# Eight row buffers and a new order for the first eight units in a linear-attention and feed-forward kernel

## The chip, the cores and the metric

The kernel runs on one core of one Trainium2 chip. The metric is the device time of one execution in microseconds (us). A core has engines that run side by side and wait for each other by semaphores: TensorE (PE, matmuls; its weight loads are listed as PEld), VectorE (DVE), ScalarE (ACT), GpSimd (POOL) and SyncE (SP, which only issues transfers here). Every engine works its own instructions off in the order in which the program has them, so an instruction that waits holds up all that stand behind it on that engine.

## The reference

There are two parts. The first is a linear attention with a decaying state: per batch b (4) and head h (8), over 768 steps of 48 channels, with a decay w per channel and a bonus u for the present step. The second is a feed-forward layer with a SiLU between two matrices of 384 x 2048 and 2048 x 384, on all 3072 tokens.

```python
for t in range(S):
    kt, vt, rt = (k[:, :, t].copy(), v[:, :, t].copy(), r[:, :, t].copy())
    cur = np.einsum('bhd,bhe->bhde', u[None] * kt, vt)
    y[:, :, t] = np.einsum('bhd,bhde->bhe', rt, state + cur)
    state = w[None, :, :, None] * state + np.einsum('bhd,bhe->bhde', kt, vt)
...
h = x @ w_in
g = h * (1.0 / (1.0 + np.exp(-h)))
return (g @ w_out).astype(np.float32)
```

## The kernel before

The sequence is cut into six chunks of 128 steps. A *unit* is one chunk of one batch, 24 in all; units 0 to 3 are chunk 0 of the four batches, 4 to 7 chunk 1, and so on. One unit loads the rows of r, k and v (three transfers), turns r and k on TensorE, multiplies them by powers of the decay on VectorE (`rT`, `kT`), forms their product (the 128 x 128 scores of eight heads), masks it (`am`), multiplies it by v (`yp`), adds the bonus part (`vu`) while it leaves PSUM, and updates the state of its batch. When the four batches of a chunk are done, the chunk passes through the feed-forward layer: `hps` is the first layer, `gT` its SiLU, `ops` the second layer.

The row buffers, the loads and the PSUM tiles:

```python
    NIN = 4

    ...
        return divmod(i, B)

    att = [ps.tile([128, 2, 512], FP, name=f"att{i}") for i in range(2)]
    turns = []

    def next_att():
        turns.append(0)
        return att[len(turns) % 2]

    ...
    u_bc = cst.tile([128, H, D], FP)
    rin = [big.tile([128, H, 64], FP, name=f"rin{i}") for i in range(NIN)]
    kin = [big.tile([128, H, 64], FP, name=f"kin{i}") for i in range(NIN)]
    vin = [big.tile([128, H, D], FP, name=f"vin{i}") for i in range(NIN)]
    ...
    wout = big.tile([128, NFT, HD], F16)

    def ld(i, dst, src, eng=nc.sync):
        sc, b = unit(i)
        eng.dma_start(
```

A load of rows is cut into runs of 48 numbers. The first transfers, the zero matmuls (`spin`, they write zeros over a tile that is about to be used and only keep TensorE busy) and the way in which u reaches all partitions:

```python
    columns(nc.sync, wpT, w, 1)
    columns(nc.scalar, wpT, w, 0)
    nc.scalar.dma_start(out=u_row, in_=bass.AP(tensor=u.tensor, offset=0, ap=[[0, 1], [1, HD]]))
    nc.scalar.dma_start(out=w_row, in_=bass.AP(tensor=w.tensor, offset=0, ap=[[0, 1], [1, HD]]))
    for i in range(B):
        for dst, src in ((rin, r), (kin, k), (vin, v)):
            ld(i, dst, src, nc.scalar if i < 2 and dst is kin else nc.sync)
    nc.vector.memset(ones, 1.0)
    ...
    spins = [0]

    def spin(ps_tile):
        for _ in range(spins[0]):
            nc.tensor.matmul(ps_tile, idle[:, 0:128], idle[:, 0:ps_tile.shape[-1]],
                             start=True, stop=True)
        spins[0] = 0
    ...

    def spread_row(key, row):
        spread[key] = ps.tile([128, HD], FP, name="bc", tag="moe", bufs=4)
        nc.tensor.matmul(spread[key], ones, row, start=True, stop=True)
    ...
    def copy_u():
        nc.scalar.copy(out=u_bc.rearrange("p h d -> p (h d)"), in_=spread["u"])
        nc.scalar.copy(out=maskX[0:HC, :], in_=maskM[HC:C, :])
        nc.scalar.copy(out=maskX[HC:C, :], in_=maskM[0:HC, :])
```

The bonus is the sum over channels of r times k times u, times v. `bonus_ku` and `bonus_rku` are on GpSimd, `bonus_sum` on VectorE; `bonus_v_rows` is used for units 0 to 3, `bonus_v` for the others:

```python
    def bonus_ku(i):
        L(i)["ku"] = wrk.tile([128, H, D], FP, name="ku")
        nc.gpsimd.tensor_tensor(out=L(i)["ku"], in0=kin[i % NIN][:, :, 0:D], in1=u_bc, op=ALU.mult)

    def bonus_rku(i):
        L(i)["rku_f"] = wrk.tile([128, H, D], FP, name="rku_f")
        nc.gpsimd.tensor_tensor(out=L(i)["rku_f"], in0=rin[i % NIN][:, :, 0:D], in1=L(i)["ku"],
                                op=ALU.mult)

    def decayed_k(i):
        nc.gpsimd.tensor_tensor(out=kc[i % NIN][:, :, 0:D], in0=kin[i % NIN][:, :, 0:D],
                                in1=lamC, op=ALU.mult)

    def bonus_v_rows(i):
        L(i)["vu"] = wrk.tile([128, H, D], FP, name="vu")
        nc.vector.tensor_tensor(out=L(i)["vu"], in0=vin[i % NIN],
                                in1=L(i)["rku"].unsqueeze(2).broadcast_to([128, H, D]),
                                op=ALU.mult)
    ...
    def bonus_v(i):
        L(i)["vu"] = wrk.tile([128, H, D], FP, name="vu")
        nc.gpsimd.tensor_tensor(out=L(i)["vu"], in0=vin[i % NIN],
                                in1=L(i)["rku"].unsqueeze(2).broadcast_to([128, H, D]),
                                op=ALU.mult)
    ...
    def turn_one(i, x):
        if x == 0:
            t = next_att()
            spin(t[:, 0, :])
            L(i)["t"] = t.rearrange("p y (x g t) -> p y x g t", x=2, g=NP)
        else:
            spin(L(i)["t"][:, 0, 1].rearrange("p g t -> p (g t)"))
        flat = (rin, kin)[x][i % NIN].rearrange("p h d -> p (h d)")
        for p in range(NP):
            for y in range(2):
                rows = slice(HC * y, HC * y + HC)
                nc.tensor.transpose(L(i)["t"][0:PR, y, x, p, :], flat[rows, 128 * p:128 * p + PR],
                                    ident[rows, rows])

    ...
        L(i)[key] = wrk.tile([PR, NP, C], FP, name=key)
        nc.vector.tensor_tensor(
            out=L(i)[key].rearrange("p g (y t) -> p y g t", y=2),
            in0=L(i)["t"][0:PR, :, x], in1=lam.rearrange("p g (y t) -> p y g t", y=2),
            op=ALU.mult)
```

The product, the mask, the output, the state and the first layer. All PSUM tiles with the tag "moe" (`bc`, `yp`, `sp`, `yT`, `hps`, `ops`) rotate through four buffers; the two `att` tiles are used in turn:

```python
    def product(i):
        at = next_att()
        spin(at[:, 0, :])
        a = L(i)["a"] = at.rearrange("p j (g c) -> p j g c", g=NP)
        rT, kT = L(i)["rT"], L(i)["kT"]
        for p in range(NP):
            for j, r0 in ((0, 0), (1, 64)):
                nc.tensor.matmul(a[:, j, p, :], kT[r0:r0 + D, p, :], rT[r0:r0 + D, p, :],
                                 start=True, stop=True)
    ...
        nc.vector.tensor_tensor(
            out=am.rearrange("p h g c -> p (h g) c"), in0=L(i)["a"].rearrange("p h g c -> p (h g) c"),
            in1=(maskX if crossed(i) else maskM).unsqueeze(1).broadcast_to([128, H, C]), op=ALU.mult)
    ...
        yp = ps.tile([128, 512], FP, name="yp", tag="moe", bufs=4)
        spin(yp)
        L(i)["y"] = yp[:, 0:HD].rearrange("p (h d) -> p h d", h=H)
    ...
        L(i)["sp"] = ps.tile([128, 512], FP, name="sp", tag="moe", bufs=4)
        L(i)["sps"] = L(i)["sp"][:, 0:HD].rearrange("p (g n) -> p g n", g=NP)
        kf = kc[i % NIN].rearrange("p h d -> p (h d)")
        vf = L(i)["v16"].rearrange("p h d -> p (h d)")
        for p in range(NP):
            nc.tensor.matmul(L(i)["sps"][:, p, :], kf[:, 128 * p:128 * p + 128],
                             vf[:, PW * p:PW * p + PW], start=True, stop=True)
    ...
        nc.vector.tensor_tensor(out=L(i)["y16"], in0=L(i)["y"], in1=L(i)["vu"], op=ALU.add)
    ...
            if sc:
                nc.vector.tensor_tensor(out=dst, in0=src,
                                        in1=L(i)["sdec"][p0:p0 + D, :, c0:c0 + D], op=ALU.add)
            else:
                nc.scalar.copy(out=st16[b][p0:p0 + D, :, c0:c0 + D], in_=src)
                nc.scalar.copy(out=dst, in_=src)
    ...
        hps = hpss[b0, ft] = ps.tile([128, m, nb * C], FP, name="hps", tag="moe", bufs=4)
        spin(hps.rearrange("p m c -> p (m c)"))
        for f in range(m):
            for q in range(NQ):
                nc.tensor.matmul(hps[:, f, :], win[:, q, (ft + f) * 128:(ft + f + 1) * 128],
                                 xts[sc][:, q, b0:b0 + nb, :].rearrange("p b t -> p (b t)"),
                                 start=(q == 0), stop=(q == NQ - 1))
    ...
        nc.scalar.activation(out=gts[sc][:, ft:ft + m, b0 * C:(b0 + nb) * C], in_=hpss[b0, ft],
                             func=AF.Silu)
```

The first eight units follow a written list, in which every word is one of the steps above with the number of its unit (`TR`, `TK`: turn r, k; `ku`, `ru`, `rd`: the three steps of the bonus; `S`: the state's matmuls; `yT`, `xT`: turn the output for the feed-forward layer and copy it; `L0.4`, `G0.4`: first layer and SiLU of batches 0 and 1 from column block 4 on, a *piece* of six matmuls; `L2.4`: the same for batches 2 and 3; `i_q`, `i_o`: one quarter of a weight matrix; `sd`: state times decay; `8*` ahead of a step: eight zero matmuls). The loop after it takes two units a turn and fills the gaps with matmuls of the feed-forward layer:

```python
    steps = {
        "lnw": powers_r, "eK": exponents_k, "lamK": powers_k,
        "wb": lambda: spread_row("w", w_row), "ub": lambda: spread_row("u", u_row),
        "lnwb": ln_w, "lamC": powers_c, "ubc": copy_u,
    }
    ...
    order = """
        lnw 5*TR0 eK lamK rT0 8*TK0 v160 ub kT0 A0 ubc i_q0 v161 wb am0 ku0 TR1 lnwb TK1 lamC
        rT1 Y0 i_q1 kT1 ru0 lr4 4*A1 v162 i_q2 rd0 TR2 vu0 TK2 kc0 lk4 lv4 y160 am1 ku1 yT0 S0
        xT0 st0 ru1 lr5 kT2 2*Y1 rT2 1*TR3 kc1 lk5 rd1 1*A2 vu1 lv5 ku2 S1 y161 st1 ru2 lr6 am2
        yT1 xT1 kc2 lk6 rd2 3*Y2 L0.0 vu2 lv6 sd4 S2 G0.0 y162 L0.2 sd5 st2 rT3 yT2 L0.4 ku3 TK3
        G0.2 L0.6 kT3 G0.4 ru3 lr7 L0.8 G0.6 A3 i_q3 rd3 G0.8 vu3 xT2 i_o0 TR4 v163 am3 TK4 kc3
        lk7 lv7 L0.10 v164 kT4 G0.10 Y3 kc4 S3 y163 st3 TR5 rT4 ku4 yT3 TK5 rT5 xT3 ru4 r164
        L2.0 kT5 r165 L2.2 kc5 rd4 G2.0 A45 G2.2 vu4 ku5 L2.4 am4 L2.6 G2.4 ru5 am5 Y4 G2.6 S4
        sd6 L0.12 v165 y164 L2.8 sd7 st4 TR6 i_o1 G0.12 rd5 Y5 S5 G2.8 rT6 TK6 vu5 L0.14 st5
        r166 i_o2 L2.10 G0.14 y165 i_o3 kT6 G2.10 L2.12 v166 kc6 TR7 TK7 G2.12 rT7 L2.14 ku6 kT7
        r167 yT4 yT5 G2.14 ru6 xT4 xT5 kc7 rd6 vu6 ku7 ru7 stb4 rd7 stb5 vu7 v167
    """
    for word in order.split():
        if "*" in word:
    ...
    load(8)
    load(9)
    fillers.extend([lambda ft=ft: l1(1, 0, 2, ft) for ft in range(0, NFT, 2)])
    fillers.extend(second(0))

    for i in range(B + 2, NU, 2):
        sc, b = unit(i)
        nxt = range(i + 2, min(i + 4, NU))
        product_pair(i)
        for n in nxt:
            bonus_products(n)
            decayed_k(n)
        masked(i)
        masked(i + 1)
        fill(4)
        outputs(i)
        evict_y(i)
        turn_y_dma(i)
        state(i)
        state16(i)
        fill(2)
        outputs(i + 1)
        evict_y(i + 1)
        turn_y_dma(i + 1)
        state(i + 1)
        state16(i + 1)
        if b:
            fillers.extend((first(sc) if sc > 1 else rest_first(sc)) + second(sc))
        fill(2)
        for n in nxt:
            turn(n)
            decay(n)
        load(i + NIN)
        load(i + 1 + NIN)
        for n in nxt:
            bonus_sum(n)
            cast_v(n)
            bonus_v(n)
            decayed_state(n)
        for n in nxt:
            fill(2)
            cast_r(n)
        fill(4)
    fill(len(fillers))
```

Of the kernel before, what the change touches and what calls it, by code (L numbers as in the profile page):

```python
# [8 lines left out]
FP = mybir.dt.float32  # L9
# [6 lines left out]
def kernel(  # L16
# [11 lines left out]
    nc = tc.nc  # L28
# [12 lines left out]
    NIN = 4  # L41
# [56 lines left out]
    u_row = cst.tile([1, HD], FP)  # L98
# [7 lines left out]
    nc.scalar.dma_start(out=u_row, in_=bass.AP(tensor=u.tensor, offset=0, ap=[[0, 1], [1, HD]]))  # L106
    nc.scalar.dma_start(out=w_row, in_=bass.AP(tensor=w.tensor, offset=0, ap=[[0, 1], [1, HD]]))
    for i in range(B):
        for dst, src in ((rin, r), (kin, k), (vin, v)):
            ld(i, dst, src, nc.scalar if i < 2 and dst is kin else nc.sync)  # L110
    nc.vector.memset(ones, 1.0)
    for i in range(NIN):
        nc.vector.memset(rin[i][:, :, D:64], 0.0)
        nc.vector.memset(kin[i][:, :, D:64], 0.0)
# [32 lines left out]
    spins = [0]  # L147

    def spin(ps_tile):
        for _ in range(spins[0]):  # L150
            nc.tensor.matmul(ps_tile, idle[:, 0:128], idle[:, 0:ps_tile.shape[-1]],  # L151
                             start=True, stop=True)
        spins[0] = 0
# [16 lines left out]
    def spread_row(key, row):  # L170
        spread[key] = ps.tile([128, HD], FP, name="bc", tag="moe", bufs=4)
        nc.tensor.matmul(spread[key], ones, row, start=True, stop=True)  # L172
# [10 lines left out]
    def copy_u():  # L183
        nc.scalar.copy(out=u_bc.rearrange("p h d -> p (h d)"), in_=spread["u"])  # L184
# [25 lines left out]
    def bonus_v_rows(i):  # L210
        L(i)["vu"] = wrk.tile([128, H, D], FP, name="vu")
        nc.vector.tensor_tensor(out=L(i)["vu"], in0=vin[i % NIN],
                                in1=L(i)["rku"].unsqueeze(2).broadcast_to([128, H, D]),
                                op=ALU.mult)

# [22 lines left out]
    def turn_one(i, x):  # L238
        if x == 0:
            t = next_att()  # L240
            spin(t[:, 0, :])
            L(i)["t"] = t.rearrange("p y (x g t) -> p y x g t", x=2, g=NP)
        else:
            spin(L(i)["t"][:, 0, 1].rearrange("p g t -> p (g t)"))
# [27 lines left out]
    def product(i):  # L272
        at = next_att()
        spin(at[:, 0, :])
        a = L(i)["a"] = at.rearrange("p j (g c) -> p j g c", g=NP)
# [27 lines left out]
    def outputs_y(i):  # L303
        sc, b = unit(i)
        yp = ps.tile([128, 512], FP, name="yp", tag="moe", bufs=4)
        spin(yp)
# [84 lines left out]
    def l1_mm(sc, b0, nb, ft):  # L391
        m = B // nb
        hps = hpss[b0, ft] = ps.tile([128, m, nb * C], FP, name="hps", tag="moe", bufs=4)
        spin(hps.rearrange("p m c -> p (m c)"))
# [60 lines left out]
    def piece(word, f):  # L455
# [5 lines left out]
        "wb": lambda: spread_row("w", w_row), "ub": lambda: spread_row("u", u_row),  # L461
        "lnwb": ln_w, "lamC": powers_c, "ubc": copy_u,
# [114 lines left out]
```

## Time and profile before

| | before |
|---|---|
| time, median of 3 runs | 200.68 us (200.18 to 200.75) |
| span of the profiled execution | 199.0 us |
| TensorE busy | 188.1 us, 2254 matmuls |
| VectorE, ScalarE, GpSimd busy | 102.6, 107.9, 117.7 us |
| rows of r and k, v: from issue to landing, median | 3.6 and 3.8 us |
| w_in and w_out, one quarter: from issue to landing, median | 6.5 and 8.2 us |

The page of the profile shows one execution. Its busy row gives the busy time of each engine, its share of the span and the number of instructions. A second part cuts the span into 40 slices and gives the busy tenths of each. A third lists the DMA queues with packets, megabytes and their share of 16 DMA engines. A fourth follows the chain of work that ended last back to the beginning. A fifth lists groups of instructions: line of the kernel, engine, operation, output and inputs, shape, count, busy time, mean time of one in ns, and the idle time of the engine just ahead of them with what ended it. From the trace behind the page one can also ask for windows of time, and for the instructions in order of time (start, duration, engine, line, operation). The ends of matmuls are modelled, and waits are inferred from semaphore events.

### The profile page before, as it was taken

What the parts mean: (1) busy time and instruction counts of PE and PEld (TensorE: products, weight loads), DVE (VectorE), ACT (ScalarE), POOL (GpSimd) and SP (SyncE); (2) the same over time, 40 slices, a digit from 0 to 9 for tenths busy, and PEclk for the clock granted to TensorE, in tenths of its full rate; (3) what the DMA queues carried; (4) which work ended last, traced back from release to release, by engine and by line L of the source; (5) the groups of instructions that cost most, each with busy time, mean ns of one, the idle gap of its engine ahead of it and who ended that gap; (6) DMA issues with size and microseconds to landing.
All of it is one profiled execution on the core that took longest, in us unless ns stands there. A gap on an engine that the chain in (4) does not pass through costs nothing.

```text
span 199.0 us, 5520 instructions
## 1 busy us (share of the span) xinstructions
PE 188.1 (95%) x2254; PEld 122.4 (61%) x2254; DVE 102.6 (52%) x176; ACT 107.9 (54%) x216; POOL 117.7 (59%) x151
## 2 busy tenths in 40 slices
PE   5899798989799999999999999999999999999992
PEld 2466476878676688666646756547665566644551
DVE  6229979673772782763564554646635625000121
ACT  5255478678572076073794355792436880179300
POOL 8079897889989919839839649569468030000000
PEclk9999999999999999999999999999999999999999
DMA  5999999899149258279175386291395102310022
GB/s 97 238 186 199 198 198 185 173 165 180 16 94 245 83 127 172 65 156 219 26 145 113 82 187 174 46 199 38 85 216 141 40 3 59 104 40 0 0 79 79
DMA packets 89981, 24.15 MB, mean 121 GB/s; under 512 B 83298, under 2 KB 89956, under 8 KB 89956
## 3 DMA queue, kind: packets, MB, share of 16 engines
q1 hardware_dynamic: 83952, 20.26, 46.7%
q0 software_dynamic: 3712, 3.15, 10.5%
q10 hardware_dynamic: 2292, 0.40, 1.0%
q8 instruction: 17, 0.28, 0.6%
q14 instruction: 8, 0.07, 0.1%
HBM read 20.45 MB, written 4.72 MB: 126 GB/s over the span
## 4 chain that ended last, share of the span: by engine, by line
PE 76%; POOL 16%; issue 4%; DVE 1%; ACT 1%; POOLq 0%; DVEq 0%
PE ops L418 32%; PE hps L397 25%; PE att L292 6%; PE att L249 5%; POOL kc L207 4%; POOL ku L199 4%; POOL rku_f L203 2%; PE yp L315 2%; POOL sdec L338 2%; PE yp L310 2%; PE bc L172 2%; POOL wout L89 2%; PE sp L327 1%; PE att L279 1%; PE att L151 1%
## 5 line engine op out<-in xcount | busy, mean ns | idle before, releaser
L397 PE MATMUL hps<-xT,win 128*128 128x256 f16 (+1 forms) x384 | 66.9, 326 | 0.4 <-ACT xT L385 0.4
L418 PE MATMUL ops<-wout,gT 128*128 128x384 f16 x384 | 65.8, 326 | 0.0
L405 ACT ACTIVATE gT<-hps 128x512 f16<-128x512 f32 x96 | 55.0, 604 | 18.3 <-PE hps L397 16.2
L418 PEld LDWEIGHTS <-gT 128*128 128x128 f16 x384 | 36.2, 98 | 23.1
L397 PEld LDWEIGHTS <-win 128*128 128x128 f16 x384 | 35.8, 98 | 23.0 <-issue 0.4
L299 DVE TENSOR_TENSOR am<-att,maskM 128x1024 f16<-128x1024 f32 x14 | 17.1, 1222 | 35.1 <-PE att L292 31.9
L424 ACT COPY osb<-ops 128x384 f32<-128x384 f32 x20 | 9.6, 480 | 45.2 <-PE ops L418 45.2
L223 POOL TENSOR_TENSOR vu<-vin,rku 128x384 f32<-128x384 f32 x20 | 16.5, 830 | 28.8 <-DVE rku L218 22.2
L199 POOL TENSOR_TENSOR ku<-kin,u_bc 128x384 f32<-128x384 f32 x24 | 24.4, 1018 | 5.8 <-ACT u_bc L184 5.4
L203 POOL TENSOR_TENSOR rku_f<-rin,ku 128x384 f32<-128x384 f32 x24 | 24.5, 1019 | 1.8
L207 POOL TENSOR_TENSOR kc<-kin,lamC 128x384 f16<-128x384 f32 x24 | 24.0, 1003 | 0.7 <-ACT wCT L180 0.7
L255 DVE TENSOR_TENSOR rT<-att,lamR 112x512 f32<-112x512 f32 x24 | 16.5, 686 | 11.6 <-PE att L249 7.4
L343 DVE TENSOR_TENSOR y<-yp,vu 128x384 f16<-128x384 f32 x24 | 13.3, 556 | 13.1 <-POOL ku L199 4.7
L255 DVE TENSOR_TENSOR kT<-att,lamK 112x512 f32<-112x512 f32 x24 | 16.3, 680 | 3.5 <-PE att L249 3.5
L292 PEld LDWEIGHTS att<-rT,kT 48*64 48x64 f32 x640 | 14.5, 133 | 3.3 <-issue 2.8
L292 PE MATMUL att<-rT,kT 48*64 48x64 f32 (+1 forms) x640 | 16.1, 247 | 0.0
L426 DVE COPY osb<-ops 128x384 f32<-128x384 f32 x4 | 2.2, 558 | 25.0 <-PE ops L418 25.0
L218 DVE TENSOR_REDUCE rku<-rku_f 128x8 f32<-128x384 f32 x24 | 12.4, 543 | 3.5 <-POOL rku_f L203 3.5
L338 POOL TENSOR_TENSOR sdec<-st,wCT 112x384 f32<-112x384 f32 x16 | 13.5, 846 | 0.4 <-ACT st L358 0.4
L270 ACT CAST rT<-rT 112x512 f16<-112x512 f32 x20 | 12.4, 623 | 0.9 <-DVE rT L255 0.8
L315 PEld LDWEIGHTS <-am 128*128 128x128 f16 x192 | 9.7, 98 | 4.8 <-DVE am L299 3.2
L299 DVE TENSOR_TENSOR am<-att,maskX 128x1024 f16<-128x1024 f32 x10 | 12.1, 1214 | 0.0
(63 smaller groups left out, 179.3 us busy)
## 6 DMA issues: line engine op xcount, KB each, us to landing
rin<-in_r_dram SPq DMA_DIRECT2D x24, 192.0 KB, 3.6
vin<-in_v_dram SPq DMA_DIRECT2D x24, 192.0 KB, 3.8
out_dram<-osb SPq DMA_DIRECT2D x24, 192.0 KB, 2.7
kin<-in_k_dram SPq DMA_DIRECT2D x22, 192.0 KB, 3.6
win<-in_moe_w_in_dram POOLq DMA_DIRECT2D x4, 384.0 KB, 6.5
wout<-in_moe_w_out_dram POOLq DMA_DIRECT2D x4, 384.0 KB, 8.2
kin<-in_k_dram ACTq DMA_DIRECT2D x2, 192.0 KB, 4.8
xT<-y SPq DMA_TRANSPOSE x18, 2.3
```

Of the source, the lines that this page charges most:

```text
L199: nc.gpsimd.tensor_tensor(out=L(i)["ku"], in0=kin[i % NIN][:, :, 0:D], in1=u_bc, op=ALU.mult)
L203: nc.gpsimd.tensor_tensor(out=L(i)["rku_f"], in0=rin[i % NIN][:, :, 0:D], in1=L(i)["ku"], op=ALU.mult)
L207: nc.gpsimd.tensor_tensor(out=kc[i % NIN][:, :, 0:D], in0=kin[i % NIN][:, :, 0:D], in1=lamC, op=ALU.mult)
L223: nc.gpsimd.tensor_tensor(out=L(i)["vu"], in0=vin[i % NIN], in1=L(i)["rku"].unsqueeze(2).broadcast_to([128, H, D]), op=ALU.mult)
L255: nc.vector.tensor_tensor(out=L(i)[key].rearrange("p g (y t) -> p y g t", y=2), in0=L(i)["t"][0:PR, :, x], in1=lam.rearrange("p g (y t) -> ...
L292: nc.tensor.matmul(a[e][o0:o0 + HC, j, p, c0:C], kT[r0:r0 + D, p, s0:s0 + HC], rT[r0:r0 + D, p, c0:C], start=True, stop=True)
L299: nc.vector.tensor_tensor(out=am.rearrange("p h g c -> p (h g) c"), in0=L(i)["a"].rearrange("p h g c -> p (h g) c"), in1=(maskX if crossed ...
L315: nc.tensor.matmul(L(i)["y"][:, h, :], L(i)["am"][:, j, p, :], L(i)["vy"][:, h, :], start=not sc, stop=(not sc or j == 1))
L338: nc.gpsimd.tensor_tensor(out=L(i)["sdec"], in0=st[b], in1=wCT.unsqueeze(2).broadcast_to([PR, NP, PW]), op=ALU.mult)
L397: nc.tensor.matmul(hps[:, f, :], win[:, q, (ft + f) * 128:(ft + f + 1) * 128], xts[sc][:, q, b0:b0 + nb, :].rearrange("p b t -> p (b t)"), ...
L405: nc.scalar.activation(out=gts[sc][:, ft:ft + m, b0 * C:(b0 + nb) * C], in_=hpss[b0, ft], func=AF.Silu)
L418: nc.tensor.matmul(opss[b], gts[sc][:, ft, b * C:(b + 1) * C], wout[:, ft, :], start=(ft == 0), stop=(ft == NFT - 1))
```

## The change

The first eight units are put into a new order, with what it needs:

- There are eight row buffers instead of four, so the rows of units 4 to 7 are asked for right after those of units 0 to 3, without waiting for a buffer, and ahead of the weights. The padding columns of the four new buffers are zeroed by copies on ScalarE.
- u is loaded to all 128 partitions by the transfer itself, instead of one row that a matmul spreads and a copy evicts.
- v times bonus is on GpSimd for all units.
- Zero matmuls write a PSUM tile of their own, so that they wait for no reader of the tile that follows.
- In the list, the steps of units 0 to 3 stand first, with the decayed k and the states after all four; nearly all pieces of the first layer come behind the fourth unit's output. Four first-layer pieces of chunk 1 (`H0` to `H3`) are moved from the loop's fillers into the list, and the bonus sums of units 6 and 7 are moved into the first turn of the loop.

The core of the diff:

```diff
-    NIN = 4
+    NIN = 8
...
-    nc.scalar.dma_start(out=u_row, in_=bass.AP(tensor=u.tensor, offset=0, ap=[[0, 1], [1, HD]]))
+    nc.scalar.dma_start(out=u_bc, in_=bass.AP(tensor=u.tensor, offset=0,
+                                              ap=[[0, 128], [D, H], [1, D]]))
...
-            ld(i, dst, src, nc.scalar if i < 2 and dst is kin else nc.sync)
+            by_act = (i == 0 and dst is vin) or (i == 1 and dst is kin)
+            ld(i, dst, src, nc.scalar if by_act else nc.sync)
...
-    for i in range(NIN):
+    for i in range(B):
...
-    spins = [0]
-
-    def spin(ps_tile):
-        for _ in range(spins[0]):
-            nc.tensor.matmul(ps_tile, idle[:, 0:128], idle[:, 0:ps_tile.shape[-1]],
-                             start=True, stop=True)
-        spins[0] = 0
+    def pads():
+        for i in range(B, NIN):
+            for dst in (rin, kin):
+                nc.scalar.copy(out=dst[i][:, :, D:64],
+                               in_=idle[:, 0:128].rearrange("p (h d) -> p h d", h=H))
+
+    def spin(n):
+        zs = ps.tile([128, 512], FP, name="zs", tag="moe", bufs=4)
+        for _ in range(n):
+            nc.tensor.matmul(zs, idle[:, 0:128], idle, start=True, stop=True)
...
-    def copy_u():
-        nc.scalar.copy(out=u_bc.rearrange("p h d -> p (h d)"), in_=spread["u"])
+    def cross_mask():
...
-    def bonus_v_rows(i):
-        L(i)["vu"] = wrk.tile([128, H, D], FP, name="vu")
-        nc.vector.tensor_tensor(out=L(i)["vu"], in0=vin[i % NIN],
-                                in1=L(i)["rku"].unsqueeze(2).broadcast_to([128, H, D]),
-                                op=ALU.mult)
...
-            t = next_att()
-            spin(t[:, 0, :])
-            L(i)["t"] = t.rearrange("p y (x g t) -> p y x g t", x=2, g=NP)
-        else:
-            spin(L(i)["t"][:, 0, 1].rearrange("p g t -> p (g t)"))
+            L(i)["t"] = next_att().rearrange("p y (x g t) -> p y x g t", x=2, g=NP)
...
-        "vu": lambda i: bonus_v_rows(i) if i < B else bonus_v(i),
+        "vu": bonus_v,
...
-        lnw 5*TR0 eK lamK rT0 8*TK0 v160 ub kT0 A0 ubc i_q0 v161 wb am0 ku0 TR1 lnwb TK1 lamC
-        rT1 Y0 i_q1 kT1 ru0 lr4 4*A1 v162 i_q2 rd0 TR2 vu0 TK2 kc0 lk4 lv4 y160 am1 ku1 yT0 S0
-        xT0 st0 ru1 lr5 kT2 2*Y1 rT2 1*TR3 kc1 lk5 rd1 1*A2 vu1 lv5 ku2 S1 y161 st1 ru2 lr6 am2
-        yT1 xT1 kc2 lk6 rd2 3*Y2 L0.0 vu2 lv6 sd4 S2 G0.0 y162 L0.2 sd5 st2 rT3 yT2 L0.4 ku3 TK3
-        G0.2 L0.6 kT3 G0.4 ru3 lr7 L0.8 G0.6 A3 i_q3 rd3 G0.8 vu3 xT2 i_o0 TR4 v163 am3 TK4 kc3
-        lk7 lv7 L0.10 v164 kT4 G0.10 Y3 kc4 S3 y163 st3 TR5 rT4 ku4 yT3 TK5 rT5 xT3 ru4 r164
-        L2.0 kT5 r165 L2.2 kc5 rd4 G2.0 A45 G2.2 vu4 ku5 L2.4 am4 L2.6 G2.4 ru5 am5 Y4 G2.6 S4
-        sd6 L0.12 v165 y164 L2.8 sd7 st4 TR6 i_o1 G0.12 rd5 Y5 S5 G2.8 rT6 TK6 vu5 L0.14 st5
-        r166 i_o2 L2.10 G0.14 y165 i_o3 kT6 G2.10 L2.12 v166 kc6 TR7 TK7 G2.12 rT7 L2.14 ku6 kT7
-        r167 yT4 yT5 G2.14 ru6 xT4 xT5 kc7 rd6 vu6 ku7 ru7 stb4 rd7 stb5 vu7 v167
+        lnw eK lamK pads lr4 lk4 lv4 lr5 lk5 lv5 lr6 lk6 lv6 lr7 lk7 lv7 10*T0 ku0 kT0 rT0 v160
+        ru0 5*A0 rd0 ku1 am0 T1 wb v161 ru1 lnwb lamC kT1 rT1 1*Y0 vu0 rd1 T2 i_q0 y160 A1 vu1
+        yT0 xT0 v162 ku2 am1 kT2 rT2 ru2 4*Y1 y161 2*A2 yT1 xT1 i_q1 rd2 vu2 v163 T3 am2 ku3 kT3
+        rT3 Y2 L0.0 y162 ru3 A3 i_q2 L0.2 G0.0 yT2 G0.2 xT2 rd3 am3 vu3 kc0 Y3 L0.4 G0.4 y163
+        kc1 L0.6 G0.6 yT3 kc2 S0 st0 xT3 i_q3 kc3 L2.0 G2.0 L2.2 G2.2 S1 st1 L2.4 G2.4 L2.6 G2.6
+        ku4 mx S2 st2 L0.8 G0.8 L0.10 G0.10 S3 st3 ru4 T4 kT4 rT4 v164 r164 L2.8 G2.8 L2.10
+        G2.10 rd4 ku5 i_o0 vu4 T5 kT5 rT5 r165 v165 A45 ru5 kc4 sd4 L0.12 G0.12 am4 L0.14 G0.14
+        am5 kc5 rd5 vu5 sd5 Y4 S4 y164 L2.12 G2.12 st4 Y5 S5 y165 L2.14 G2.14 st5 yT4 xT4 stb4
+        stb5 i_o1 T6 kT6 rT6 yT5 xT5 ku6 ru6 i_o2 kc6 v166 r166 H0 H1 H2 T7 kT7 rT7 i_o3 H3 r167
+        v167 ku7 ru7 kc7 sd6 sd7
...
+        elif word[0] == "H":
+            l1(1, 0, 2, 2 * int(word[1]))
...
-    fillers.extend([lambda ft=ft: l1(1, 0, 2, ft) for ft in range(0, NFT, 2)])
+    fillers.extend([lambda ft=ft: l1(1, 0, 2, ft) for ft in range(8, NFT, 2)])
...
-        for n in nxt:
-            bonus_products(n)
-            decayed_k(n)
+        if i > B + 2:
+            for n in nxt:
+                bonus_products(n)
+                decayed_k(n)
         masked(i)
         masked(i + 1)
+        if i == B + 2:
+            for n in (i, i + 1):
+                bonus_sum(n)
+                bonus_v(n)
+            for n in nxt:
+                bonus_products(n)
+                decayed_k(n)
...
-        load(i + NIN)
-        load(i + 1 + NIN)
+        load(i + B)
+        load(i + 1 + B)
```

## The prediction

> **What bounds the kernel now.** I read the page's busy row first, then its 40 slices, then two windows, and last the instructions in order of time.
>
> ```profile
> PE 188.1 (95%) x2254; PEld 122.4 (61%) x2254; DVE 102.6 (52%) x176; ACT 107.9 (54%) x216; POOL 117.7 (59%) x151
> ...
> PE   5899798989799999999999999999999999999992
> ...
> DMA  5999999899149258279175386291395102310022
> ...
> PE 76%; POOL 16%; issue 4%; DVE 1%; ACT 1%; POOLq 0%; DVEq 0%
> ```
>
> TensorE is the bound, but not everywhere. Each digit stands for 5 us: from the 12th slice on PE reads 9 without a break, in the first eleven it dips, and there the DMA row reads 9. The windows cut at the first second-layer matmul (57.2 us) say the same; columns after the stretch and its length are busy us of PE, PEld, DVE, ACT and POOL, the clock share, the DMA share and GB/s:
>
> ```profile
> 4.58:57.20 52.62, 47.52 (x649) 35.62 (x649) 35.11 (x53) 33.00 (x74) 42.85 (x47) 1.00 0.96 169
> 57.20:199.00 141.80, 138.30 (x1604) 86.14 (x1600) 64.38 (x108) 72.59 (x140) 70.98 (x86) 1.00 0.45 105
> ```
>
> After 57.2 us nothing can be won by the change: it leaves that work alone and PE is full (the missing 3.5 us are the last store). So the question is how early the full stretch begins. What PE must do before it, at durations of the full stretch: ten units of transposes at 0.52 (5.2 us), four single products at 1.16 (4.6), two pairs at 1.5 (3.0), outputs and states of eight units (4.3), six y transposes (1.0), 24 first-layer pieces at 0.66 (15.8), the row spread (0.8): about 35 us. PE takes 57.2. So some 22 us of the start are waiting, zero matmuls and slow matmuls; more than 4 of them precede the first rows.
>
> The order of time shows three causes:
>
> ```profile
> 10.09 2.08 PE L279 MATMUL att<-rT,kT 48*128 48x128 f32 x16
> ...
> 16.84 1.46 PE L279 MATMUL att<-rT,kT 48*128 48x128 f32 x16
> ...
> 21.13 1.16 PE L279 MATMUL att<-rT,kT 48*128 48x128 f32 x16
> ...
> 31.95 0.37 PE L315 MATMUL yp<-v,am 128*128 128x48 f16 x8 [0.20 <-DVE am L299]
> ```
>
> The same 16 matmuls cost 2.08, 1.46 and 1.16 us: PE is slow until about 17 us, though the page's clock row shows 9 throughout. And unit 3's output matmuls (the last line) come only at 31.95 us, against 14.70 for unit 0. From 15 to 50.5 us the chain of waits runs nearly all through GpSimd: kc, ku, rku_f, sdec and the weight issues, one after another.
>
> [...] vu on VectorE takes 0.78 to 1.50 us (mean 1.17), on GpSimd 0.83 each time. [...]
>
> **The change, part by part.** The costs used, from the groups of the first 57 us (last columns: busy us, mean ns, idle before):
>
> ```profile
> L405 ACT ACTIVATE gT<-hps 128x512 f16<-128x512 f32 x24 | 14.0, 597 | 7.9 <-PE hps L397 7.6
> ...
> L199 POOL TENSOR_TENSOR ku<-kin,u_bc 128x384 f32<-128x384 f32 x10 | 10.4, 1035 | 5.4 <-ACT u_bc L184 5.4
> ...
> L299 DVE TENSOR_TENSOR am<-att,maskM 128x1024 f16<-128x1024 f32 x6 | 7.3, 1219 | 4.9 <-PE att L279 3.2 <-PE att L292 1.7
> L255 DVE TENSOR_TENSOR rT<-att,lamR 112x512 f32<-112x512 f32 x9 | 6.2, 687 | 4.9 <-PE att L249 3.9 <-ACT gT L405 1.0
> ```
>
> *Start.* u is loaded to all partitions (about 0.2 MB more, near 0.8 us at the 250 GB/s seen from 5 to 10 us) instead of a PE spread of 1.64 and an ACT copy of 0.48. It shares the DMA with r of unit 0, which I put at 5.1 us instead of 4.5; k and v of unit 0 follow at 6.8. The ten zero matmuls have their own tile and no rT to wait for: about 0.46 us each, from 1.3 to 5.8. Then r transposes, k transposes at 6.8 to 7.2, five zero matmuls warm to 8.3, kT and rT to 8.9, and the first product at **9.0 instead of 10.09**, in 1.16 instead of 2.08: 10.2 against 12.17.
>
> *Units 0 to 3.* Per unit the cycle is product 1.2 with its semaphore, am 1.2, the two decays 1.3 on VectorE, then the next product: 3.8 us. The reductions and y evictions fit beside the product. Products at 9.0, 12.7, 16.5, 20.2; am of unit 3 ends near 22.7, so **its output matmuls come at 22.7 instead of 31.95**. GpSimd keeps pace: per unit ku, rku_f, vu (0.83, moved here) and a weight issue 0.8 make 3.7. But fewer pieces are behind: at that point before, six first-layer pieces, unit 4's transposes and three states were done; here two pieces and none of the rest. The lead is about 9 us, less 4 us of work owed.
>
> *The debt is paid on ScalarE.* From the third piece to the y copies of units 4 and 5 it has 14 silus (14 x 0.59 = 8.2), four state evictions of four copies (1.08 each, 4.3), three xT copies (1.4), the mask halves (0.6), and casts for units 4 and 5 (3.3): 17.8 us. It begins at 23.7 and waits some 2.5 us, once for the second pair's y, once behind the pair product: **to 44.1**. All PSUM tiles but att rotate through four buffers, so PE cannot run ahead; it has only some 13 us of work there and stands for the rest. At 44.1 PE has done about 24.7 of its 35 us.
>
> *GpSimd after that.* The sum for unit 5 stands behind both am's on VectorE, so vu of unit 5 starts at 40.3. After it in order: four decays or casts, three wout issues (2.4), products and kc of units 6 and 7 (6), the vu's (1.7): vu of unit 7 near 55. The y eviction of unit 6 waits for its own vu to 54.4, just when PE wants that buffer (54.7): 0.3 us of wait. The last wout part is issued at 48.9 and should land by 55, as it is wanted.
>
> *Sum.* The old kernel is full from 52.3 with 29.4 us of its start work done. The new one has 24.7 at 44.1, needs 4.7 more, and loses 0.7 waiting for rT of unit 7 and 0.3 above: 49.9. The gain is **2.4 us**. The span becomes 196.6; the time has lain 1.7 above the span: **198.3**, rounded to 198.2.
>
> **Rivals.** *PE warms late.* Zero matmuls alone did not warm it by 10 us before; if ten do not either, products stay at 2.08 to the second unit and most of the lead at 10 us is gone: gain 1, near 199.7. For it: eight zero matmuls at 6.1 us did nothing. Against: they ran 1.86 us and were followed by matmuls over one row; here PE is busy from 1.3 to 6.4 almost without a gap.
>
> *Weights arrive too late.* Rows of four more units now go first and w_in's first part is issued at 11.7 instead of 4.5. With its 6.5 us to landing it is there at 18.3, needed at 19.3.
>
> ```profile
> q1 hardware_dynamic: 83952, 20.26, 46.7%
> q0 software_dynamic: 3712, 3.15, 10.5%
> ```
>
> Against it: a weight packet holds an engine 90 ns (10.5% of 199 us times 16, by 3712), a row packet 18[...]. If they land at 22 instead, 2 us are lost: near 200.
>
> *ScalarE is less of a bound than I count* (more silus fall into the waits of units 2 and 3, or the first products come a microsecond earlier): gain 4, near 196.7.
>
> *GpSimd becomes the bound of the pair loop.* It comes out of the first eight units 2 us later against PE than now. For it: busy 71 of 141.8 us and in order. Against: that leaves half of each 14.3 us pair.
>
> **Range and chances.** The rivals spread the gain from about 0 to 4. I take 198.2 us, 196.2 to 200.4 for eight in ten. Faster by over 2% means below 196.7, a gain of 4 us that only the third rival gives: 0.13. Slower by over 2% would need new waits of 4 us beyond all lost gains: 0.02. The rest is 0.85.
>
> **What would show it.** First product at 8.5 to 9.5 us and 1.2 us long; if 2 us, the clock step is wrong. Unit 3's output matmuls at 22 to 24. From 24 to 43 us ScalarE busy over 85% and PE under 75%, PE's waits naming ScalarE; if PE waits for DMA there, the weights were it. vu of unit 5 at about 40. PE full from about 49, then as before, with pairs at 14.3 us. The prediction is wrong if a wait on GpSimd's vu holds PE after 52 us, if the loop's pitch grows, or if PE is full well before 47.

## The result and the profile after the change

The changed kernel takes 197.95 us (median, 197.84 to 198.3), the kernel before 200.56 us beside it (200.18 to 200.75): a ratio of 0.9875, with a 95% interval of 0.9855 to 0.9895. The span fell from 199.0 to 196.6 us. Prediction: 198.2 us, a span of 196.6.

The page of the changed kernel: busy time, three rows of the 40 slices, and the chain of waits by engine.

```profile
PE 182.9 (93%) x2250; PEld 119.9 (61%) x2250; DVE 97.8 (50%) x172; ACT 109.8 (56%) x223; POOL 120.5 (61%) x159
...
PE   7697868789989999999999999999999999999992
...
PEclk9999999999999999999999999999999999999999
DMA  3999999968939549259149268176287201410022
...
PE 76%; ACT 6%; DVE 6%; POOL 5%; DMA 3%; issue 2%; SPq 0%; POOLq 0%; DVEq 0%
```

TensorE has 5.2 us less to do (182.9 instead of 188.1: the spread of u and the slow matmuls of the first units are gone) and still stands idle 2.8 us more (13.7 of the span instead of 10.9). Its row dips to 6, 7 and 8 between 25 and 44 us, the debt the prediction spoke of. GpSimd's share of the chain went from 16 to 5%; ScalarE and VectorE, 1% each before, now have 6% each.

The windows of the changed kernel, cut at its first second-layer matmul (columns as before: stretch, length, busy us of PE, PEld, DVE, ACT and POOL, clock, DMA share, GB/s):

```profile
4.58:52.07 47.49, 39.43 (x595) 31.06 (x594) 27.62 (x43) 33.61 (x80) 38.07 (x47) 1.00 1.07 186
52.07:196.60 144.53, 140.13 (x1652) 87.64 (x1649) 67.22 (x115) 74.13 (x141) 78.60 (x94) 1.00 0.46 105
```

The second layer starts 5.1 us earlier, but the stretch behind it grew from 141.8 to 144.5 us. It holds 48 matmuls more: the outputs and the state of unit 7 and the transposes of units 8 and 9 now come behind the cut. (24 pieces of the first layer stand ahead of it in both kernels.) The gain is the 2.4 us that are left. It can be seen right behind those transposes, first in the kernel before, then in the changed one:

```profile
57.23 2.94 PE L418 MATMUL ops<-wout,gT 128*128 128x384 f16 x17
```

```profile
57.38 2.94 PE L407 MATMUL ops<-wout,gT 128*128 128x384 f16 x17
```

Both kernels stand there at nearly the same time, but the changed one has already done 16 second-layer matmuls (at 52.07 and 54.95 us, about 0.16 us each), the kernel before none. So the pair loop is not earlier: the masks of units 8 and 9 start at 64.30 us (64.15 before), those of the last pair at 163.7 (163.5). It has fewer fillers left, and the gain comes out at its end.

The changed kernel's instructions in order of time (start, length, engine, line, tile; the bracket holds the idle time before it and what ended it; lines between these are left out) show the new start and every later wait of TensorE that counts:

```profile
9.02 1.16 PE L270 MATMUL att<-rT,kT 48*128 48x128 f32 x16 [0.27 <-DVE rT L248]
...
12.71 1.16 PE L270 MATMUL att<-rT,kT 48*128 48x128 f32 x16
...
22.56 0.38 PE L305 MATMUL yp<-v,am 128*128 128x48 f16 x8 [0.40 <-DVE am L290]
26.39 1.47 PE L386 MATMUL hps<-xT,win 128*128 128x256 f16 x12 [1.80 <-ACT xT L375]
32.33 1.47 PE L386 MATMUL hps<-xT,win 128*128 128x256 f16 x12 [0.60 <-ACT st L348]
35.78 1.55 PE L283 MATMUL att<-rT,kT 48*64 48x128 f32 x60 [1.02 <-DVE rT L248]
40.71 0.33 PE L317 MATMUL sp<-v,kc 128*128 128x96 f16 x4 [0.33 <-DVE y L333]
43.30 2.12 PE L386 MATMUL hps<-xT,win 128*128 128x256 f16 x18 [0.57 <-ACT xT L375]
47.40 1.55 PE L283 MATMUL att<-rT,kT 48*64 48x128 f32 x60 [0.26 <-DVE rT L248]
54.78 0.33 PE L317 MATMUL sp<-v,kc 128*128 128x96 f16 x4 [0.86 <-DVE y L333]
```

The first product takes 1.16 us instead of 2.08, and unit 3's outputs (22.56) come 9.4 us earlier than before. The waits after that name ScalarE (its copies xT and st) three times, and VectorE (rT, y) four times. None names a DMA. The last bracket is the late one: the y of unit 6, which itself waited for GpSimd.

### The profile page after: what moved, and what is told of

Read it like the earlier page. It is cut to its first block, busy times and chain, and to the rows that moved or that the text cites. A ratio compares the mean times of both kernels' runs of the same rounds, so it can differ in the third digit from the quotient of the medians.

```text
span 196.6 us, 5505 instructions
## 1 busy us (share of the span) xinstructions
PE 182.9 (93%) x2250; PEld 119.9 (61%) x2250; DVE 97.8 (50%) x172; ACT 109.8 (56%) x223; POOL 120.5 (61%) x159
## 4 chain that ended last, share of the span: by engine, by line
PE 76%; ACT 6%; DVE 6%; POOL 5%; DMA 3%; issue 2%; SPq 0%; POOLq 0%; DVEq 0%
PE ops L407 32%; PE hps L386 26%; PE att L283 6%; PE att L242 5%; DMA kin<-in_k_dram 3%; PE att L270 2%; DVE am L290 2%; ACT gT L394 2%; PE yp L305 2%; PE yp L300 1%; PE sp L317 1%; DVE rT L248 1%; DVE kT L248 1%; ACT stb L347 1%; POOL ku L202 1%
## 5 line engine op out<-in xcount | busy, mean ns | idle before, releaser
L386 PE MATMUL hps<-xT,win 128*128 128x256 f16 (+1 forms) x384 | 67.7, 326 | 3.0 <-ACT xT L375 2.4
L220 POOL TENSOR_TENSOR vu<-vin,rku 128x384 f32<-128x384 f32 x24 | 19.8, 829 | 31.2 <-DVE rku L215 27.8
L248 DVE TENSOR_TENSOR kT<-att,lamK 112x512 f32<-112x512 f32 x24 | 16.4, 682 | 14.2 <-PE att L242 14.2
L283 PE MATMUL att<-rT,kT 48*64 48x128 f32 (+1 forms) x640 | 16.5, 248 | 1.3 <-DVE rT L248 1.3
L229 ACT CAST v<-vin 128x384 f16<-128x384 f32 x24 | 11.5, 513 | 2.2 <-DMA vin<-in_v_dram 2.2
```

What stands on the lines that cost most here:

```text
L220: nc.gpsimd.tensor_tensor(out=L(i)["vu"], in0=vin[i % NIN], in1=L(i)["rku"].unsqueeze(2).broadcast_to([128, H, D]), op=ALU.mult)
L248: nc.vector.tensor_tensor(out=L(i)[key].rearrange("p g (y t) -> p y g t", y=2), in0=L(i)["t"][0:PR, :, x], in1=lam.rearrange("p g (y t) -> ...
L283: nc.tensor.matmul(a[e][o0:o0 + HC, j, p, c0:C], kT[r0:r0 + D, p, s0:s0 + HC], rT[r0:r0 + D, p, c0:C], start=True, stop=True)
```

## The experiments

All times stand beside runs of the kernel before on the same chip. "The changed kernel" is always the one above, at 0.9875. Its executions, and those of its variants, scatter in part because TensorE turns fast at different moments: in the new order with ten or sixteen zeros in front, the first product starts at 8.72 to 9.24 us in eight profiles and at 10.10 and 10.12 in two. Below this is called the switch of the clock. The name is an inference: the page's clock row reads 9 all through the start, but where it reads 5, in one slice of the kernel with early weights, four zero matmuls take 1.92 us instead of 1.03. The stretch of a profile from unit 3's outputs to its end leaves the start out: it is 174.0 us in the changed kernel (196.6 less 22.56). It is 174.0 as well in the profiles of the four variants that change only what stands ahead of it (no zeros, sixteen zeros, the bonus on VectorE, early weights). For the other variants it is given below, from one profile each.

**The clock, first: no zero matmuls.** The theory was that the early start rests on the zero matmuls that make TensorE fast (1.16 us for a product instead of 2.08); the rival, that other work does so anyway.

```diff
-  10*T0 ...   5*A0 ...   1*Y0 ...   4*Y1 ...   2*A2
+     T0 ...     A0 ...     Y0 ...     Y1 ...     A2
```

> The changed kernel without any of its 22 zero matmuls. My account: TensorE is slow until the work of units 0 to 2 has warmed it; two or three products at about 2.1 us instead of 1.16, transposes doubled; unit 3's output matmuls at 25 to 26 us instead of 22.6; everything behind shifts by the same, so 200 to 201 us, all of the gain lost. Rival, that the order of the steps alone makes the gain and the clock warms by itself: within 0.5 us of 197.95, unit 3's outputs by 23.2.

Measured: 202.91 us, ratio 1.0095 (1.0073 to 1.0118): the new order without its zero matmuls is slower than the kernel before. The loss is larger than I had expected. The order of time of that kernel, products of units 0 to 3:

```profile
9.49 2.08 PE L270 MATMUL att<-rT,kT 48*128 48x128 f32 x16 [1.45 <-DVE rT L248]
...
15.25 2.02 PE L270 MATMUL att<-rT,kT 48*128 48x128 f32 x16
...
19.80 2.08 PE L270 MATMUL att<-rT,kT 48*128 48x128 f32 x16 [0.69 <-DVE rT L248]
...
24.80 1.16 PE L270 MATMUL att<-rT,kT 48*128 48x128 f32 x16
```

and its window between the first product and the last one:

```profile
10.00:24.00 14.00, 12.41 (x131) 9.85 (x127) 8.65 (x14) 4.78 (x9) 9.93 (x12) 1.00 1.09 195
```

TensorE is listed as busy for 12.41 of 14 us and stays slow all that time (2.02 and 2.08 us for a product, 0.63 to 0.68 for eight transposes that take 0.39 to 0.44 in the changed kernel); the clock column says 1.00. Unit 3's outputs come at 27.29 us, and every later event stands 4.7 us behind the changed kernel's (the pair product at 40.50 instead of 35.78). So 22 matmuls that compute nothing carry 4.7 us of span, all of it ahead of unit 3's outputs.

**Zero matmuls alone, in the old order.** The kernel before, with its zeros in a tile of their own and ten of them in front; order, buffers and the spread of u stay old.

```diff
-  lnw 5*TR0 eK lamK rT0 8*TK0 ...
+  lnw 10*TR0 eK lamK rT0 8*TK0 ...
+  zs = ps.tile([128, 512], FP, name="zs", tag="moe", bufs=4)
```

> The kernel before with its zero matmuls in a tile of their own and ten instead of five in front, the order untouched. My account: first product at 9.0 to 10.2 us and warm, so the chain through GpSimd starts 1 to 2 us earlier and keeps that: 199.2 to 200.2 us, up to half of the gain. Rival, that the gain is all in the order: within 0.3 us of before.

Measured: 199.35 us, ratio 0.9921 (0.9897 to 0.9945), as expected. Its first product, in the order of time, and GpSimd's `ku` and `kc` of unit 0:

```profile
9.12 1.16 PE L272 MATMUL att<-rT,kT 48*128 48x128 f32 x16
```

```profile
9.71 0.99 POOL L196 TENSOR_TENSOR ku<-kin,u_bc 128x384 f32<-128x384 f32 x1 [4.29 <-ACT u_bc L181]
...
13.26 1.01 POOL L204 TENSOR_TENSOR kc<-kin,lamC 128x384 f16<-128x384 f32 x1
```

The spread of u runs on TensorE too (0.91 us here, 1.64 before), so the earlier switch brings the `ku` of unit 0 forward from 10.76 to 9.71 us; unit 3's outputs come at 29.89 instead of 31.95. By the medians, about six tenths of the gain (0.79 of 1.25%) need none of the reordering. Whether the tile of their own or the larger number of zeros does it was not tried apart. In the changed kernel u comes by a transfer of its own and the `ku` of unit 0 starts at 7.14 us; no run has that part of the change alone.

**More zeros.** Sixteen instead of ten in front of the changed kernel (`10*T0` becomes `16*T0`).

> Sixteen zero matmuls instead of ten in front; r of unit 0 lands only at about 6.3 us, so they fit. Two executions of kernels with this start (10 zeros) had the first product at 10.1 us, two at 8.7 to 9.0, and the run times fall in two groups 1.3 us apart. My account, that a gap in the zeros before 6.4 us lets the clock switch later: all executions early, median 197.5 to 197.9 and no time above 198.4. Rival, that the two groups have nothing to do with the gap: both groups stay, or, if the zeros now run past the rows, 0.3 us slower.

Measured: 198.41 us (198.16 to 198.5), ratio 0.9874 (0.9855 to 0.9892). A miss: it is no faster. The zeros are a clock of their own: ten slow ones take 4.45 us and five 2.32, five fast ones 1.25. In the changed kernel's profile ten took 3.93, and 4.21 in that of the kernel with all changes together, so the switch came within them; in four others the ten took 4.45, but the first transposes, at 6.1 to 6.6 us, were fast (0.43 to 0.49 us for eight). In two of the experiments below (sum of unit 5, bonus on VectorE) those transposes took 0.68 and the five 2.32, and the switch came only at about 10.1. Sixteen fill the wait for the first rows (TensorE's first product is at 9.17) and gain nothing where ten were enough. These four executions lie within 0.34 us of each other; four are too few to say that a late switch can no longer happen.

**The buffers.** First the old order with `NIN = 8` and nothing else; then the new order with `NIN = 4`, each load of units 4 to 7 placed behind the last reader of its buffer.

```diff
-    NIN = 4        # first kernel: old order
+    NIN = 8
-    NIN = 8        # second kernel: new order; lr4 behind ru0, lv4 behind vu0, lk4 behind kc0, and so on
+    NIN = 4
```

> The kernel before with eight row buffers and nothing else. My account: rows were never what the old order waited for after its first microseconds, GpSimd's row of work was; 200.3 to 200.9 us against 200.7, no difference. Rival, that earlier rows are a large part of the gain: 1 us or more faster.

> The new order with four row buffers; the loads of units 4 to 7 are issued as soon as the old rows have been read (r after rku_f, v after vu, k after kc), and the padding copies on ScalarE fall away. My account: k of unit 4 is loaded from about 23 us, lands by 27 and is wanted by GpSimd at 26.5 and by TensorE at 31: 0 to 0.6 us slower than 197.95. Rival, that the eight buffers carry the gain: 1.5 us or more slower, with GpSimd or TensorE waiting for rows.

Measured: 0.9999 (0.9986 to 1.0013) for the buffers alone, and 0.9914 (0.9889 to 0.9938; 199.31 us) for the order without them. Eight buffers are worth nothing by themselves. To the new order they are worth something near 0.8 us by the ratios, a little over the 0 to 0.6 expected, though the interval overlaps that of the changed kernel; in the profile the stretch behind unit 3's outputs is 0.4 us longer (174.4). The wait they take away, in the order of time of the four-buffer kernel:

```profile
32.09 0.43 PE L242 MATMUL att<-ident,kin 64*112 64x64 f32 x8 [0.74 <-DMA kin<-in_k_dram]
32.12 1.01 POOL L202 TENSOR_TENSOR ku<-kin,u_bc 128x384 f32<-128x384 f32 x1 [5.75 <-DMA kin<-in_k_dram]
```

GpSimd stands 5.75 us for k of unit 4, whose buffer is free only after kc of unit 0. Most of that falls where it has nothing urgent; TensorE sees 0.74.

**The bonus of units 0 to 3 back on VectorE** (`"vu": lambda i: bonus_v_rows(i) if i < B else bonus_v(i)`).

> v times bonus of units 0 to 3 back on VectorE, the rest as changed. My account, a cycle of product, mask and decays with VectorE full beside it: 0.8 to 1.2 us more per unit, unit 3's outputs at 25 to 26 us, time 199.4 to 200.4. Rival, that where vu runs does not matter in the new order because the reductions wait for GpSimd anyway: within 0.5 us.

Measured: ratio 0.9958 (0.9938 to 0.9978), about 200.0 us beside 200.89. Five of its 14 executions took 204.2 to 205.0 us, at a mean clock of 0.973 to 0.988 against 0.991 to 1.0 for the others, and are not in that ratio. The time lies within the expectation, but in part by luck. The unit cycle grew only from 3.7 to about 4.0 us (products at 10.12, 13.87, 18.05, 22.21), and unit 3's outputs come at 24.70, not at 25 to 26. From the first product to there the move costs 1.0 us (14.58 instead of 13.54), some 0.3 per unit instead of the 0.8 to 1.2 expected. The other 1.1 us by which this profile is late are its clock, which switched only at about 10.1 (first product at 10.12 instead of 9.02).

**The first weights ahead of the first product** (`i_q0` from behind T2 to the front of GpSimd's row).

> The changed kernel with the first part of w_in issued by GpSimd ahead of its first product (0 instead of about 12 us), so that weights share the DMA with the rows of units 0 and 1. Theory (rows ahead of weights are needed for the early start): the first product comes at 9.5 to 11 us instead of 9.0, unit 3's outputs at 23.5 to 24.5 instead of 22.6, and the time is 198.6 to 200, half to two us over the changed kernel. Rival (the rows are ahead anyway because they are issued by then, and ScalarE sets the rest): unit 3's outputs stay at 22.6 to 23 and the time within 0.4 of 197.95.

Measured: 199.41 us, ratio 0.9929 (0.9907 to 0.9951): 1.1 us over the changed kernel's ratio, as expected. In the profiled execution the path was another one. The first product stayed at 8.90; the rows of unit 2 were late instead, and unit 3's outputs came at 25.74:

```profile
12.70 0.44 PE L242 MATMUL att<-ident,rin 64*112 64x64 f32 x8 [0.83 <-DMA rin<-in_r_dram]
13.50 0.68 PE L242 MATMUL att<-ident,kin 64*112 64x64 f32 x8 [0.36 <-DMA kin<-in_k_dram]
13.96 2.02 PE L270 MATMUL att<-rT,kT 48*128 48x128 f32 x16
```

In the changed kernel these transposes start at 11.92 and wait for nothing. Here TensorE was also slow again behind the two waits (2.02 us for the second product, 1.92 for the four zeros behind it), and this time the page's clock row shows it, with 8 and 5 tenths in the third and fourth slices (10 to 20 us):

```profile
PEclk9985999999999999999999999999999999999999
```

That execution took 201.41 us at a mean clock of 0.983; the other six took 199.16 to 199.56 at 0.996 to 0.998, so nothing of that length happened in them. Their spans of 197.5 to 197.8 us, less the same 174.0, put unit 3's outputs at 23.5 to 23.8 (an estimate), as expected.

**ScalarE as the bound of the middle.** The 16 state copies of chunk 0 (4.3 us of ScalarE) go to VectorE, which had 8.2 us with nothing to do from 23.6 to 31.8 us.

```diff
-  nc.scalar.copy(out=st16[b][p0:p0 + D, :, c0:c0 + D], in_=src)
-  nc.scalar.copy(out=dst, in_=src)
+  nc.vector.tensor_copy(out=st16[b][p0:p0 + D, :, c0:c0 + D], in_=src)
+  nc.vector.tensor_copy(out=dst, in_=src)
```

> The 16 state copies of units 0 to 3 (4.3 us of ScalarE) go to VectorE, which does nothing from 24 to 31.8 us. My account, ScalarE as the bound from 24 to 43 us: the pair product of units 4 and 5 starts about 2.2 us earlier than 35.8, vu of unit 5 near 38 instead of 40.3, time 195.8 to 196.6. Rival, that GpSimd (or the weights' landing) is the bound of that stretch: under 0.4 us.

Measured: 197.11 us, ratio 0.981 (0.978 to 0.9839), the interval wholly under the changed kernel's; span 194.8. Windows from 24 to 43 us, first the changed kernel, then this one:

```profile
24.00:43.00 19.00, 14.97 (x244) 12.79 (x242) 8.52 (x15) 16.07 (x41) 12.93 (x16) 1.00 1.07 194
```

```profile
24.00:43.00 19.00, 16.08 (x256) 13.76 (x253) 14.39 (x32) 13.53 (x27) 14.40 (x18) 1.00 1.07 194
```

TensorE does 1.1 us more in the same stretch, and of its waits for ScalarE the first falls from 1.80 to 0.72 us (xT) and the second, 0.60 for st, is gone. So ScalarE did hold it. But 4.3 us off ScalarE bought 1.3 us by the ratios (1.5 in the profile behind unit 3's outputs, 172.5 instead of 174.0), where the expected times meant 1.35 to 2.15: it was a bound together with others. The wait for rT of the pair product is now 1.22 us instead of 1.02, and the y of unit 6 still held TensorE for 0.89.

**The sum of unit 5 ahead of the masks** (`rd5` from behind `am5 kc5` to behind `sd4`).

> Only the bonus sum of unit 5 moves, ahead of the two masks on VectorE, where it fits without cost. My account: vu of unit 5 starts near 38 instead of 40.3, GpSimd's row of work behind it ends 2 us earlier, and TensorE's wait of 0.9 us for the y eviction of unit 6 at 53.9 us is gone: 0.8 to 1.1 us faster, near 197.0. Rival, that GpSimd after 40 us is hidden: no difference (under 0.3 us).

Measured: 198.05 us (197.64 to 199.11), ratio 0.9859 (0.9827 to 0.9891): by the times not to be told from the changed kernel. But this profile is of an execution whose clock switched late (199.01 us; first product at 10.10, unit 3's outputs at 23.72 instead of 22.56), and behind that point it is 0.5 us shorter (173.6 instead of 174.0 us). TensorE's wait for the y of unit 6 is 0.43 us instead of 0.86, and the one of 0.33 at 40.71 is gone. So the move gains about half of what was expected. GpSimd's row in its order of time shows where the rest went:

```profile
39.22 0.82 POOL L220 TENSOR_TENSOR vu<-vin,rku 128x384 f32<-128x384 f32 x1
40.01 0.82 POOL L328 TENSOR_TENSOR sdec<-st,wCT 112x384 f32<-112x384 f32 x1
42.11 0.50 POOL L353 CAST stb<-st 112x384 f16<-112x384 f32 x1 [1.29 <-DVE st L344]
43.33 0.51 POOL L353 CAST stb<-st 112x384 f16<-112x384 f32 x1 [0.72 <-DVE st L344]
```

The bonus of unit 5 comes 1.05 us earlier although this execution started 1.16 late; two instructions later GpSimd waits 1.29 and 0.72 us for the states of units 4 and 5, and most of its lead is lost there.

**All of it together.** State copies on VectorE, the early sum of unit 5, and the sum and bonus of unit 6 ahead of the pair product of units 6 and 7:

```diff
-  T7 kT7 rT7 i_o3 H3 r167 v167 ku7 ru7 kc7 sd6 sd7
+  T7 kT7 rT7 rd6 i_o3 H3 r167 v167 ku7 vu6 ru7 kc7 sd6 sd7
-            for n in (i, i + 1):
+            for n in (i + 1,):
```

> The changed kernel with the state copies of chunk 0 on VectorE (which alone took 0.8 us off), the bonus sum of unit 5 ahead of the two masks, and sum and bonus of unit 6 ahead of the pair product of units 6 and 7. Theory (after the copies left ScalarE, GpSimd's row behind the bonus of unit 5 sets when PE gets full, and its last items hold the y of unit 6): the bonus of unit 6 ends by 49 instead of 53.3, PE's wait of 0.9 us for y of unit 6 goes, and the time is 195.8 to 196.8. Rival (PE is short of PSUM buffers in any case until about 50 us): within 0.4 of 197.1, what the copies alone gave.

Measured: 195.79 us (195.64 to 197.14), ratio 0.9766 (0.9737 to 0.9795), span 194.1: faster than both kernels, and as the theory had it. Its waits by engine, TensorE's three longest over the whole span (waiter, what it waits for, us in total, times, longest):

```profile
PE att L283 <- DVE rT L248: 1.5, 2, 1.2
PE zs L157 <- DVE idle L102: 1.3, 1, 1.3
PE hps L386 <- ACT xT L375: 1.3, 2, 0.7
```

No line of the whole list names y: the wait of 0.86 us at 54.78 is gone, and xT costs 1.3 us instead of 2.4. Over the kernel with the state copies alone the intervals overlap slightly, so the times alone don't prove the share of the early sums. The profiles do show it: the waits for y are removed, and the stretch behind unit 3's outputs is 171.4 us instead of 172.5.

**And still earlier.** As the last kernel, with turns and decays of unit 5 right behind those of unit 4, and two weight issues moved up into GpSimd's idle time (`i_o1` ahead of `vu4`, `i_o2` ahead of `vu5`).

> As the kernel with early sums, and besides the turns and decays of unit 5 right behind those of unit 4, and two of the weight issues for w_out moved up into GpSimd's idle time before the bonuses of units 4 and 5 (they are 0.75 us each and stood in its full stretch from 42 to 52 us). Theory (GpSimd in order is the bound from 42 to 52 us): another 0.5 to 1.5 us, 194.9 to 196.0. Rival (VectorE and PSUM buffers bound it): 195.8 to 196.8, as the kernel with early sums alone.

Measured: 196.93 us (196.16 to 198.43), ratio 0.9812 (0.9775 to 0.9848). A miss: no gain, and behind unit 3's outputs the profile is 0.5 us longer than the last kernel's (171.9 instead of 171.4). The bonus of unit 4 starts at 34.51 us instead of 33.26, since its sum now stands behind two more decays on VectorE. GpSimd reaches the product for the sum of unit 5 later for that, and VectorE's row, in order of time, waits for it ahead of the masks:

```profile
36.33 0.55 DVE L215 TENSOR_REDUCE rku<-rku_f 128x8 f32<-128x384 f32 x1 [1.91 <-POOL rku_f L206]
36.80 1.22 DVE L290 TENSOR_TENSOR am<-att,maskM 128x1024 f16<-128x1024 f32 x1
```

TensorE then waits 1.04 us for the mask of unit 4. What came free on GpSimd was given back through VectorE.

**The best version with sixteen zeros** (`16*T0` in the kernel with early sums).

> As the kernel with VectorE state copies and early sums (195.79, with single executions up to 197.1), with sixteen zero matmuls ahead of the first rows instead of ten. Theory (the executions above 196.5 are those in which TensorE's clock switches only at 10 us, and a longer run of zeros puts the switch ahead of the first product in every execution): all executions at 195.5 to 196.2, median 195.9. Rival (the scatter comes from elsewhere): executions above 196.6 appear as before.

Measured: 195.64 us (195.45 to 196.75), ratio 0.9756 (0.973 to 0.9782). The same as with ten within the intervals (171.3 us behind unit 3's outputs), and one execution of five still at 196.75. So the theory that more zeros remove the scatter falls here. That execution has a mean clock of 0.991 on record, the other four 0.998 to 1.0; what lowers it is open.

## Why the prediction was right, point by point

**What bounds the kernel.** Right: the second layer and the loop went on as they were. The masks of the pairs of units 8 to 15 stand at 64.30, 78.60, 92.85 and 107.07 us, a pitch of 14.2 to 14.3, as in the kernel before. One reading was loose: in the eleventh slice TensorE's row dips, but the DMA row reads 1 there; the kernel before waited 1.38 us ahead of 52.30 for a mask.

**The start.** First product 9.0 predicted, 9.02 measured, 1.16 us long. Two terms were off and cost nothing: r of unit 0 was there at 6.38, not 5.1 (its transposes waited 1.17 us for it), and the ten zeros took 3.93 us, not 4.5, as the clock switched inside them. k at 7.13 (predicted 6.8) and the two decays behind it set the product.

**Units 0 to 3.** Products at 9.02, 12.71, 16.39 and 20.07 against 9.0, 12.7, 16.5 and 20.2; unit 3's outputs 22.56 against 22.7. The cycle of 3.8 us measured 3.7.

**The debt on ScalarE.** Its end was put at 44.1; the last of the three xT copies ends at 43.25. ScalarE is busy 16.07 of 19 us from 24 to 43 (84.6%, just under what I said), TensorE 14.97 (79%, not under 75). Of the 3.75 us of waits shown there, 2.40 name ScalarE. What I had mis-sized is how alone ScalarE was: I had TensorE "stand for the rest" of 17.8 us of ScalarE work, and taking 4.3 of that away gave 1.3. The rT of the pair product (1.02 us) and the y evictions are VectorE's.

**GpSimd after that.** vu of unit 5 at 40.3 predicted, 40.27 measured; vu of unit 7 ends at 54.92 ("near 55"). The y of unit 6 was put at 54.4 and a wait of 0.3: it starts at 54.17, ends 0.56 later, and TensorE waited 0.86, as it was there earlier than I had it. The wait for rT of unit 7 was 0.26, not 0.7. The two errors nearly cancel: 1.12 against 1.0 in all. The prediction had also named a wait for GpSimd's vu after 52 us as a sign of being wrong, although its own sum held 0.3 us of it. By that sign it was wrong here: the path was foreseen, its size was nearly three times as large.

**The sum.** Gain 2.4 predicted, 2.4 measured in the span. (Its terms, 44.1, 4.7, 0.7 and 0.3, add up to 49.8, not 49.9.) It is right, but that it agrees so closely is in part luck: two of its terms came out by errors that cancelled, and the stall that it put on ScalarE alone was shared with VectorE. The prediction also named the zeros as a mere part of the start. The runs show them to be, by the medians, the larger half (0.9921 alone) and the condition of the rest (1.0095 without).

**The rivals.** *PE warms late* was close to home: where zeros are missing, everything is 4.7 us later. Without them TensorE was busy 12.41 of 14 us and still slow at the end of it (2.08 us for the product at 19.80, 0.63 for the transposes at 22.71), so a high busy share alone did not make it fast. What keeps it slow in this mix was not shown. *Weights arrive too late*: no; w_in's first piece starts at 19.09 us without a wait, and issuing earlier costs 1.1 us. *ScalarE less of a bound*: in part true, as above. *GpSimd the bound of the pair loop*: no; once the y of unit 6 is past, the order of time lists no wait of TensorE for another engine after 55 us.

## What to carry to other kernels

Ask first whether the early matmuls are slow, by the length of one shape early and late (2.08 and 1.16 us for a product here), and try filling TensorE's wait for the first rows with large matmuls (ten of 128 x 512 here, the only size tried in that place; 0.9921 in the old order). An order that depends on a fast start loses without it (1.0095). Where a list of engines takes turns as the bound, a move pays only until the next engine's wait, so look at what the freed instruction's follower waits for before moving it: one of the moves here gave back on VectorE what it had won on GpSimd, and another kept about 0.5 us of a lead of 2.2. Buffers are worth what the order that uses them can do with them: nothing in the old order (0.9999), under a microsecond in the new one (about 0.8).

## What the runs showed of the hardware

- At the start of the kernel before and of the one without zeros, the page's clock row and column said 9 and 1.00 while the same 16 matmuls took 2.08 us instead of 1.16; only the length of a matmul told. The one later slow stretch in a trace does show there: 8 and 5 tenths in two slices, 0.983 in the mean, with 2.02 us for the 16 matmuls.
- Without zeros TensorE was slow to 22.71 us at least (0.63 us for eight transposes) and fast at 24.80 (1.16 for a product), through 12.41 us of busy time in 14. Up to 23.5 us it ran only small matmuls there: transposes, products over 48 rows, outputs of 128 x 48 and one over a single row; the first piece of the feed-forward layer, at 23.60, took 1.27 us instead of 0.82.
- In eight profiles of the new order that began with ten or sixteen zero matmuls of 128 x 512 at 1.29 us, TensorE was fast by the first transposes, at 6.08 to 6.82 us (0.43 to 0.49 us for eight). In the changed kernel the zeros start 0.43 us apart up to 4.25 us and 0.22 apart from 4.62.
- When it switches varies between executions of kernels with the same start: within the ten zeros (3.93 and 4.21 us), between them and the first transposes (4.45), or, in two profiles, only at about 10.1 us (2.32 us for the five zeros before that, 1.25 and 1.22 for the product behind them). In the kernel with early weights it was slow again at about 13.5 us (0.68 us for eight transposes), behind waits of 0.83 and 0.36 us for rows; one trace shows it, and its cause wasn't tried.
